# Seating the last two token tiles and placing gathered rows: a new order on TensorE between the dense and the expert products

## The chip, the cores and the metric

The kernel runs on one core of one Trainium2 chip. The metric is the device time of one execution in microseconds (us), as a median over several runs. The profile is of one execution of its own; its times are in us unless marked ns.

## What is computed

Three layers run one after the other over 1792 tokens of 768 features: attention with head mixing, a dense two-layer network, and a mixture of eight experts. The change stands where the second ends and the third begins:

```python
skip_score = x @ w_skip
do_compute = skip_score > 0
xc = x[do_compute]
logits = xc @ w_gate
e_idx = np.argmax(logits, axis=1)
gate_w = probs[np.arange(len(xc)), e_idx]        # softmax of the logits
for e in range(E):
    mask = e_idx == e
    h = np.maximum(xc[mask] @ w1[e], 0.0)
    y[mask] = gate_w[mask, None] * (h @ w2[e])
out[do_compute] = xc + y
```

Every token that computes goes to one expert, so each expert needs the list of its tokens before its products can start.

## The kernel before

**The dense products.** The 14 token tiles of 128 rows go through `w_out` tile by tile (L918). Tile 13 is LAST. Its 16 reduction steps are cut in two column halves near the end, so that the first 512 columns of its result are ready before the last 256. ScalarE copies each half out of PSUM into `x2` (L948).

**Scoring and routing.** Tiles 0 to 12 are scored on VectorE (`score`, L805). Tile 13 is turned by TensorE (`score_turned`, L903), copied by ScalarE (L904) and multiplied with the gate weights (`logits`, L894) into `lg`. `route` (L811 to L826) finds on VectorE the best expert (`oh`, one-hot, and `do`, whether the token computes) and the softmax weight; the exponential is ScalarE's (L824).

**Seating.** `seat` gives each token its place in its expert's list. TensorE multiplies `ones` with `seen`, the counts so far (L833), and `upper` with `oh` (L835), both into `pp`. VectorE adds `oh` to `seen` (L836), reads the place out of `pp` (`ps`, `sl`, L839), makes a slot number (`big`, `slot`, `si`), and GpSimd writes the token's number and weight into the table `slots` in DRAM (L853, an indirect DMA). OLD is 12: for tiles 12 and 13 `seat` also makes `hot` (L847), a 128 by 128 matrix that puts the tile's tokens straight into the first expert's input.

**Placing.** The input of expert 0 is gathered on TensorE in the PSUM tiles `pt`, in six column blocks k: rows of the tiles before OLD, which an indirect DMA has fetched into `xp` (L923), times `ident` (L889); rows of tile 12 times its `hot` (L890); rows of tile 13 times its `hot` (L963). `place_old` issues the first two for a block together. ScalarE and VectorE split `pt` into `xt0` (L965, L966), which the first expert product (L1113) reads.

**Experts.** `whi` and `wlo` are the high and low parts of the expert weights, made by ScalarE (L1084) and VectorE (L1086) from loads that SyncE issues (L1073). The products with `w1` are L1113, the turns of `h` L1101 to L1103, the products with `w2` L1126. GpSimd reads the lists back from `slots` into `ids` (L1237 to L1242) and gathers rows with them (L1091). `plan` counts the lists; `reorder` (L1050 to L1057) exchanges lists on VectorE after `ids` has landed.

**What sets the order.** In this part a scheduler orders each engine's queue at build time, by the order of the program, by what depends on what and by its own model of durations. `behind(op)` adds an edge that puts an instruction after `op` on the same engine's queue. At run time each engine works its queue off in that order.

Of the kernel before, what the change touches and what calls it, by code (L numbers as in the profile page):

```python
# [8 lines left out]
FP32 = mybir.dt.float32  # L9
# [4 lines left out]
ALU = mybir.AluOpType  # L14
# [6 lines left out]
NK = DM // 128  # L21
NF = DFF // 128
NTILE = NT // 128
# [464 lines left out]
def mixtures(tc, order, xT, w_in, w_out, w_skip, w_gate, w1, w2, ident, gT, wf, wg, x2d, slots, out):  # L488
# [5 lines left out]
    with ExitStack() as top:  # L494
# [266 lines left out]
        with ExitStack() as ctx:  # L761
# [47 lines left out]
            def route(i, lg):  # L809
# [14 lines left out]
                nc.scalar.activation(out=ex, in_=lg[:, :E], func=ACTF.Exp, bias=nmx, accum_out=sm)  # L824
                nc.vector.tensor_scalar(out=sm, in0=sm, scalar1=1e-9, scalar2=None, op0=ALU.add)
                nc.vector.reciprocal(out=pairs[:, i, 1:2].bitcast(FP32), in_=sm)  # L826
                return i, oh, do

            def seat(i, oh, do, after=None):

                pp = ps_r.tile([128, 512], FP32, tag="r", name="pp")
                with behind(after):
                    nc.tensor.matmul(out=pp[:, :E], lhsT=ones, rhs=seen, start=True, stop=False)  # L833
                with behind(after):
                    nc.tensor.matmul(out=pp[:, :E], lhsT=upper, rhs=oh, start=False, stop=True)  # L835
# [8 lines left out]
                place = None  # L844
                if i >= OLD:
                    place = wg_p.tile([128, 128], FP32, tag=f"hot{i}", name="hot")
                    nc.vector.tensor_scalar(out=place, in0=iota128, scalar1=sl, scalar2=do, op0=ALU.is_equal,  # L847
                                            op1=ALU.mult)
                slot = st_p.tile([128, 1], FP32, tag="slot", name="slot")
# [6 lines left out]
                return place  # L856

            gs = {0: load_g(0)}
            for f0 in range(EARLY, NF, 2):
# [23 lines left out]

            def place_old(ks):

                for k in ks:
                    col = slice(k * 128, (k + 1) * 128)
                    o = pt[k // 3][:, k % 3, :]
                    nc.tensor.matmul(out=o, lhsT=xp[:, col], rhs=ident, start=(k % 3 == 0), stop=False)  # L889
                    nc.tensor.matmul(out=o, lhsT=rows[LAST - 1][:, col], rhs=old_hot, start=False, stop=False)  # L890

            def logits(turned):
                for k, t in turned:
                    nc.tensor.matmul(out=lg[:, :E + 1], lhsT=t, rhs=wgt[:, k, :], start=(k == 0), stop=(k == NK - 1))  # L894

            def score_turned(x2, c):

                ks = range(0, CUT // 128) if c == 0 else range(CUT // 128, NK)
                p = ps_o.tile([128, 4, 128], FP32, tag=f"o{c}", name="tx")
                t = st_p.tile([128, 6, 128], FP32, tag="prod", name="tx", bufs=2)  # L900
                for j, k in enumerate(ks):
                    with behind(mm):
                        nc.tensor.transpose(p[:, j], x2[:, k * 128:(k + 1) * 128], ident)  # L903
                copied = nc.scalar.copy(out=t[:, :len(ks)], in_=p[:, :len(ks)])  # L904
                return [(k, t[:, j]) for j, k in enumerate(ks)], copied

            for i, n, fc, cs in work:
# [18 lines left out]
                if last and n == len(halves) - 5:  # L926
                    turned, _ = score_turned(x2, 0)
                if last and n == len(halves) - 3:
# [5 lines left out]
                if i and n == (AT_ROUTE if last else AT_OLD if i == OLD else AT_SEAT):  # L934
                    hot = old_hot = seat(*routing, None if last else mm)
                    if i == OLD:
# [482 lines left out]
```

## Time and profile before

| | |
|---|---|
| median of 3 runs | 993.32 us (992.25 to 994.23) |
| the profiled execution | 988.09 us |
| its span | 986.2 us |
| TensorE busy in the span | 963.5 us (98%) |
| VectorE busy | 722.0 us (73%) |
| ScalarE busy | 550.9 us (56%) |
| GpSimd busy | 233.5 us (24%) |

The span runs from the first to the last record of the profiled execution; 1.9 us of its time lie around it. Busy TensorE time includes matmuls that overlap, so it doesn't say how close the engine is to its peak.

### The profile page before, as it was taken

The numbers are of one execution on the slowest core, as the hardware profiler recorded it, in microseconds if no ns is written. First come the engines' busy times: TensorE is split into PE (matmuls) and PEld (weight loads), VectorE is DVE, ScalarE is ACT, GpSimd is POOL, SyncE is SP. The second block draws the span as 40 slices with busy tenths as digits, with TensorE's granted clock in tenths as the row PEclk, the third lists the DMA queues.
The fourth block names the chain that finished last, engine by engine and source line by source line (L and its number), as shares of the span: only waits on it lengthen the run. The fifth ranks groups of instructions, "written<-read, shape, count | busy, mean of one in ns | idle before, by whom it ended". The sixth has DMA issues, their size and how long they took to land. (4 is left out here: it accounts for less than half of the span.)

```text
span 986.2 us, 30114 instructions
## 1 busy us (share of the span) xinstructions
PE 963.5 (98%) x12286; PEld 838.7 (85%) x12286; DVE 722.0 (73%) x1458; ACT 550.9 (56%) x1113; POOL 233.5 (24%) x291
## 2 busy tenths in 40 slices
PE   9999999999998999999999999999999999999996
PEld 4677777777776789998999999999999998898985
DVE  6777777777776786666666478877686847999973
ACT  4887788788786754444554453222212106788861
POOL 2333234234222322223233100010100004252001
PEclk9999999999999999999999999999999999999999
DMA  6674674574557565445666389643333387999910
GB/s 202 219 237 145 216 234 156 198 240 153 195 190 234 175 207 184 157 161 169 219 225 211 137 292 290 175 126 97 118 97 100 104 294 264 394 394 397 391 71 34
DMA packets 129160, 199.86 MB, mean 203 GB/s; under 512 B 31924, under 2 KB 95863, under 8 KB 128764
## 3 DMA queue, kind: packets, MB, share of 16 engines
q1 hardware_dynamic: 126812, 191.60, 58.1%
q0 software_dynamic: 2160, 6.31, 1.7%
q8 instruction: 97, 1.59, 0.7%
q14 instruction: 43, 0.35, 0.1%
q10 hardware_dynamic: 48, 0.00, 0.0%
HBM read 122.66 MB, written 37.35 MB: 162 GB/s over the span
## 5 line engine op out<-in xcount | busy, mean ns | idle before, releaser
L918 PE MATMUL o<-w,gh 128*128 128x384 f32 (+2 forms) x1344 | 238.2, 336 | 0.0
L636 PE MATMUL h<-xh,w 128*128 128x448 f32 x1152 | 235.4, 366 | 1.6 <-DVE xh L572 1.3
L918 PEld LDWEIGHTS o<-w,gh 128*128 128x128 f32 x1344 | 232.0, 188 | 2.2
L636 PEld LDWEIGHTS h<-xh,w 128*128 128x128 f32 x1152 | 215.7, 188 | 20.2 <-DVE xh L572 1.9
L214 DVE TENSOR_REDUCE nmx<-c 128x1 f32<-128x448 f32 x184 | 102.3, 617 | 51.9 <-PE c L206 51.8
L266 PEld LDWEIGHTS f<-kr,e 64*64 64x64 f32 x5888 | 105.3, 135 | 36.6 <-issue 22.3
L227 ACT ACTIVATE e<-c,nmx 128x448 f32<-128x448 f32 x184 | 114.5, 633 | 25.5 <-DVE nmx L214 25.4
L805 DVE SCALAR_TENSOR_TENSOR junk<-x,wrow 128x768 f32<-128x768 f32 x117 | 111.8, 955 | 18.4 <-ACT x L948 12.8
L247 POOL TENSOR_SCALAR kr<-kpost,rs 128x60 f32<-128x60 f32 x184 | 79.4, 455 | 183.9 <-DVE rs L242 90.6
L1086 DVE TENSOR_TENSOR wlo<-w1t,whi 128x1536 fp32r<-128x1536 f32 x64 | 110.8, 1751 | 10.7 <-ACT whi L1084 8.9
L266 PE MATMUL f<-kr,e 64*64 64x60 f32 (+1 forms) x5888 | 108.3, 219 | 2.9 <-issue 1.8
L553 POOL TENSOR_TENSOR wf<-a,p 128x768 f32<-128x768 f32 x32 | 66.1, 2066 | 181.1 <-DVE p L551 139.4
L1084 ACT CAST whi<-w1t 128x1536 fp32r<-128x1536 f32 x64 | 93.8, 1483 | 21.5 <-PE y L1126 9.4
L790 ACT CAST gh<-gr 128x512 fp32r<-128x512 f32 x56 | 34.8, 624 | 97.1 <-PE o L918 35.5
L206 PE MATMUL c<-d,kpre_low 64*64 64x448 f32 x368 | 84.1, 547 | 0.3 <-DMA d<-s 0.2
L206 PE MATMUL c<-d,kpre_up 60*64 60x448 f32 x368 | 81.6, 548 | 0.0
L272 ACT COPY at<-f 128x420 f32<-128x420 f32 (+1 forms) x136 | 65.6, 518 | 28.0 <-PE f L266 27.2
L294 PE MATMUL xp<-at,v 128*64 128x120 f32 (+1 forms) x1152 | 67.1, 264 | 3.1 <-issue 3.0
L853 POOL DMA_INDIRECT slots<-pairs,si x14 | 18.9, 1348 | 204.6 <-DVE si L852 152.7
L166 PE MATMUL qk<-k,qq 64*120 64x448 f32 x504 | 65.3, 381 | 0.7 <-ACT e L227 0.2
L294 PEld LDWEIGHTS xp<-at,v 128*64 128x64 f32 x1152 | 56.1, 137 | 10.6 <-issue 9.3
L170 ACT ACTIVATE s<-qk 120x448 f32<-120x448 f32 x96 | 52.2, 548 | 23.1 <-PE qk L166 14.6
(204 smaller groups left out, 1278.7 us busy)
## 6 DMA issues: line engine op xcount, KB each, us to landing
w1t<-in_moe_w_dram SPq DMA_DIRECT2D x64, 768.0 KB
d<-s SPq DMA_DIRECT2D x176, 210.0 KB
gT<-g SPq DMA_DIRECT2D x64, 224.0 KB
f<-in_moe_w_in_dram SPq DMA_DIRECT2D x16, 768.0 KB
f<-in_moe_w_out_dram SPq DMA_DIRECT2D x16, 768.0 KB
gr<-gT SPq DMA_DIRECT2D x48, 256.0 KB
rq<-in_q_dram SPq DMA_DIRECT2D x15, 360.0 KB
rk<-in_k_dram SPq DMA_DIRECT2D x24, 224.0 KB
```

Source lines behind the costliest of these rows:

```text
L206: nc.tensor.matmul(out=ps[j * UP:(j + 1) * UP, :S], lhsT=kpre_up[UP:UP + HP, :] if z else kpre_low, rhs=d[z, j])
L214: nc.vector.tensor_reduce(out=t, in_=c, op=ALU.max, axis=AX.X, negate=True)
L227: nc.scalar.activation(out=e, in_=c, func=ACTF.Exp, bias=t, accum_out=sms[0][:, k + i:k + i + 1])
L247: nc.gpsimd.tensor_scalar(out=kr, in0=kposts[z], scalar1=rs[:, 2 * i + z:2 * i + z + 1], scalar2=None, op0=ALU.mult)
L266: nc.tensor.matmul(out=ps[to, heads, z, :], lhsT=e[rows, keys * JW:(keys + 1) * JW], rhs=kr[rows, first * HR:(first + n) * HR])
L294: nc.tensor.matmul(out=ps[i][z * 64:(z + 1) * 64, :n], lhsT=vt[b, p][:, jc * 2 + z, :], rhs=att[T][:, jc * H + ORDER.index(2 * p + z), :n] ...
L553: nc.gpsimd.tensor_tensor(out=w, in0=a, in1=p, op=ALU.add)
L636: nc.tensor.matmul(out=ps, lhsT=w[:, a, kk, :], rhs=xs[tb, kk][:, z, :], start=(kk == 0 and a + z == 0), stop=(kk == NK - 1 and a == 1))
L805: nc.vector.scalar_tensor_tensor(out=t[:, o:o + n], in0=x2, scalar=1.0, in1=w, op0=ALU.mult, op1=ALU.mult, accum_out=lg[:, e:e + 1])
L918: mm = nc.tensor.matmul(out=po[c][:, :cols[c].stop - cols[c].start], lhsT=gs[i][fc // GC][:, a, fc % GC, :], rhs=wo[fc][:, z, cols[c]], st ...
L1084: nc.scalar.copy(out=hi, in_=t)
L1086: nc.vector.tensor_tensor(out=lo, in0=t, in1=hi, op=ALU.subtract)
```

## The change

`place_old` is split: `place_pre` issues the products with `ident`, `place_old` those with the `hot` of tile 12. `seat` is split: `counted` issues the product of `ones` with `seen`, and for tile 12 the rest of `seat` is called later, between the turns and the logits of the last columns of tile 13. Edges fix one order on TensorE: `place_pre` of blocks 0 and 1, the turns, `upper` of tile 12, `place_pre` of blocks 2 and 3, the logits, `place_pre` of blocks 4 and 5, `place_old` of blocks 0 and 1, both products of tile 13's seat, `place_old` of blocks 2 to 5. On VectorE the two instructions of the softmax weight (`weigh`) stand behind `hot` for tiles 12 and 13, and the addition to `seen` stands after them in the program.

```diff
-                nc.vector.tensor_scalar(out=sm, in0=sm, scalar1=1e-9, scalar2=None, op0=ALU.add)
-                nc.vector.reciprocal(out=pairs[:, i, 1:2].bitcast(FP32), in_=sm)
-                return i, oh, do
+                def weigh(after=None):
+                    with behind(after):
+                        nc.vector.tensor_scalar(out=sm, in0=sm, scalar1=1e-9, scalar2=None, op0=ALU.add)
+                    nc.vector.reciprocal(out=pairs[:, i, 1:2].bitcast(FP32), in_=sm)
+                if i < OLD:
+                    weigh()
+                return i, oh, do, weigh
+            def counted(i, oh, do, weigh, after=None):
                 pp = ps_r.tile([128, 512], FP32, tag="r", name="pp")
                 with behind(after):
                     nc.tensor.matmul(out=pp[:, :E], lhsT=ones, rhs=seen, start=True, stop=False)
+                return i, oh, do, weigh, after, pp
...
-                nc.vector.tensor_tensor(out=seen, in0=seen, in1=oh, op=ALU.add)
                 nc.vector.scalar_tensor_tensor(out=ps, in0=pp[:, :E], scalar=1.0, in1=oh, op0=ALU.mult, op1=ALU.mult,
                                                accum_out=sl)
+                place = None
+                if i >= OLD:
+                    place = wg_p.tile([128, 128], FP32, tag=f"hot{i}", name="hot")
+                    made = nc.vector.tensor_scalar(out=place, in0=iota128, scalar1=sl, scalar2=do, op0=ALU.is_equal,
+                                                    op1=ALU.mult)
+                    weigh(made)
+                nc.vector.tensor_tensor(out=seen, in0=seen, in1=oh, op=ALU.add)
...
                         if last and c == 1:
-                            turned, freed = score_turned(x2, c)
-                            place_old(range(2))
-                            logits(turned)
-                            place_old(range(2, 4))
+                            placed = place_pre(range(2), mm)
+                            turned, freed, done = score_turned(x2, c, placed)
+                            with behind(done):
+                                done = seat_old()
+                            done = place_pre(range(2, 4), done)
+                            done = logits(turned, done)
+                            done = place_pre(range(4, NK), done)
+                            done = place_old(range(2), done)
...
-            hot = seat(*route(NTILE - 1, lg))
-            place_old(range(4, NK))
+            hot = seat(*route(NTILE - 1, lg), done)
+            place_old(range(2, NK), seated[LAST])
```

## Rows read from the trace of the kernel before

**Rows 1.** The page's head: span and number of instructions.

```profile
span 986.2 us, 30114 instructions
```

**Rows 2.** Busy time by stretch: PE, PEld, DVE, ACT, POOL, then clock, DMA share, GB/s.

```profile
836.00:977.00 141.00, 141.00 (x890) 126.52 (x889) 125.19 (x137) 101.91 (x102) 35.07 (x15) 1.00 0.78 297
815.70:822.75 7.05, 6.23 (x51) 5.54 (x49) 3.33 (x33) 3.23 (x8) 1.13 (x2) 1.00 0.64 245
```

**Rows 3.** Timeline of PE from the last dense product to the first expert product.

```profile
815.70 0.61 PE L889 MATMUL pt<-ident,xp 128*128 128x128 f32 x4
816.33 0.44 PE L903 MATMUL tx<-ident,x 128*128 128x128 f32 x2
817.23 0.61 PE L894 MATMUL lg<-wgt,tx 128*128 128x9 f32 x4 [0.46 <-ACT tx L904]
817.70 0.37 PE L835 MATMUL pp<-oh,upper 128*128 128x8 f32 x2
818.33 0.39 PE L833 MATMUL pp<-seen,ones 128*128 128x8 f32 x2 [0.27 <-DVE ps L839]
...
819.78 0.61 PE L890 MATMUL pt<-hot,x 128*128 128x128 f32 x4
820.23 0.29 PE L835 MATMUL pp<-oh,upper 128*128 128x8 f32 x2
...
821.35 1.50 PE L963 MATMUL pt<-hot,x 128*128 128x128 f32 x12
822.75 1.65 PE L1113 MATMUL ph<-whi,xt 128*128 128x512 f32 x6
```

**Rows 4.** Timeline of DVE: routing and seating of tiles 12 and 13.

```profile
815.39 0.17 DVE L811 MAX8 mx<-lg 128x8 f32<-128x8 f32 x1
...
816.06 0.28 DVE L819 TENSOR_SCALAR oh<-iota,ef,do 128x8 f32<-128x8 f32 x1
...
817.88 0.17 DVE L811 MAX8 mx<-lg 128x8 f32<-128x8 f32 x1 [1.53 <-PE lg L894]
...
818.41 0.33 DVE L847 TENSOR_SCALAR hot<-iota,sl,do 128x128 f32<-128x128 f32 x1
...
818.85 0.14 DVE L852 CAST si<-slot 128x1 int32<-128x1 f32 x1
...
818.97 0.29 DVE L819 TENSOR_SCALAR oh<-iota,ef,do 128x8 f32<-128x8 f32 x1
...
820.76 0.35 DVE L847 TENSOR_SCALAR hot<-iota,sl,do 128x128 f32<-128x128 f32 x1
```

**Rows 5.** Timeline of ACT in the same stretch.

```profile
816.80 0.37 ACT L904 COPY tx<-tx 128x256 f32<-128x256 f32 x1 [0.53 <-PE tx L903]
817.07 0.30 ACT L824 ACTIVATE ex<-lg,nmx 128x8 f32<-128x8 f32 x1
```

**Rows 6.** Timeline of POOL: writing the lists and reading them back.

```profile
819.27 1.02 POOL L853 DMA_INDIRECT slots<-pairs,si  x1 [3.47 <-DVE oh L819]
822.81 0.97 POOL L853 DMA_INDIRECT slots<-pairs,si  x1 [2.51 <-DMA slots<-pairs,si]
825.21 0.61 POOL L1237 DMA_DIRECT2D ids<-slots  x1 [1.43 <-DMA slots<-pairs,si]
...
826.91 0.90 POOL L1242 DMA_DIRECT2D ids<-slots  x1
```

**Rows 7.** Timeline of DVE and PE in the first expert's products.

```profile
829.40 1.74 DVE L1086 TENSOR_TENSOR wlo<-w1t,whi 128x1536 fp32r<-128x1536 f32 x1
...
832.45 0.17 DVE L1050 TENSOR_TENSOR swapped<-ids 128x8 int32<-128x8 int32 x1 [1.24 <-DMA ids<-slots]
832.53 1.75 DVE L1086 TENSOR_TENSOR wlo<-w1t,whi 128x1536 fp32r<-128x1536 f32 x1
...
834.27 0.68 DVE L1103 TENSOR_TENSOR ht<-pt,ht 128x512 fp32r<-128x512 f32 x1
...
835.00 1.66 PE L1126 MATMUL y<-whi,ht 128*128 128x384 f32 x8 [0.71 <-DVE ht L1103]
```

**Rows 8.** Timeline of SP: the first expert weight load after the seats.

```profile
825.69 0.38 SPq L1073 DMA_DIRECT2D w1t<-in_moe_w_dram  x1
```

More of the change, by code (lines that the diff above doesn't have):

```diff
@@ L824, in route @@
                 nc.scalar.activation(out=ex, in_=lg[:, :E], func=ACTF.Exp, bias=nmx, accum_out=sm)
-                nc.vector.tensor_scalar(out=sm, in0=sm, scalar1=1e-9, scalar2=None, op0=ALU.add)
-                nc.vector.reciprocal(out=pairs[:, i, 1:2].bitcast(FP32), in_=sm)
-                return i, oh, do
-            def seat(i, oh, do, after=None):
+                def weigh(after=None):
[6 more added lines that the diff above has]
+            def counted(i, oh, do, weigh, after=None):
                 pp = ps_r.tile([128, 512], FP32, tag="r", name="pp")
@@ L833, in seat @@
                     nc.tensor.matmul(out=pp[:, :E], lhsT=ones, rhs=seen, start=True, stop=False)
+                return i, oh, do, weigh, after, pp
+            def seat(i, oh, do, weigh, after=None, pp=None):
+                if pp is None:
+                    pp = counted(i, oh, do, weigh, after)[-1]
                 with behind(after):
-                    nc.tensor.matmul(out=pp[:, :E], lhsT=upper, rhs=oh, start=False, stop=True)
-                nc.vector.tensor_tensor(out=seen, in0=seen, in1=oh, op=ALU.add)
+                    seated[i] = nc.tensor.matmul(out=pp[:, :E], lhsT=upper, rhs=oh, start=False, stop=True)
                 ps = st_p.tile([128, E], FP32, tag="ps", name="ps")
@@ L843, in seat @@
                                         op1=ALU.add)
[L844 to L848, printed above, removed]
                 slot = st_p.tile([128, 1], FP32, tag="slot", name="slot")
@@ L856, in seat @@
                 return place
+            seated, started, hots = {}, [], []
             gs = {0: load_g(0)}
@@ L882, in mixtures, with place_pre, seat_old, place_old @@
             lg = ps_r.tile([128, 512], FP32, tag="r", name="lg")
-            def place_old(ks):
+            def place_pre(ks, after):
                 for k in ks:
[L887 to L892, printed above, removed]
-                for k, t in turned:
-                    nc.tensor.matmul(out=lg[:, :E + 1], lhsT=t, rhs=wgt[:, k, :], start=(k == 0), stop=(k == NK - 1))
-            def score_turned(x2, c):
+                    with behind(after):
+                        done = nc.tensor.matmul(out=pt[k // 3][:, k % 3, :], lhsT=xp[:, k * 128:(k + 1) * 128], rhs=ident,
+                                                start=(k % 3 == 0), stop=False)
+                return done
+            def seat_old():
+                hots.append(seat(*started[0]))
+                return seated[OLD]
+            def place_old(ks, after):
+                for k in ks:
+                    with behind(after):
+                        done = nc.tensor.matmul(out=pt[k // 3][:, k % 3, :],
+                                                lhsT=rows[LAST - 1][:, k * 128:(k + 1) * 128], rhs=hots[0],
+                                                start=False, stop=False)
+                return done
+            def logits(turned, after=None):
+                for k, t in turned:
+                    with behind(after):
+                        done = nc.tensor.matmul(out=lg[:, :E + 1], lhsT=t, rhs=wgt[:, k, :], start=(k == 0),
+                                                stop=(k == NK - 1))
+                return done
+            def score_turned(x2, c, mm):
                 ks = range(0, CUT // 128) if c == 0 else range(CUT // 128, NK)
@@ L902, in score_turned @@
                     with behind(mm):
-                        nc.tensor.transpose(p[:, j], x2[:, k * 128:(k + 1) * 128], ident)
+                        done = nc.tensor.transpose(p[:, j], x2[:, k * 128:(k + 1) * 128], ident)
                 copied = nc.scalar.copy(out=t[:, :len(ks)], in_=p[:, :len(ks)])
-                return [(k, t[:, j]) for j, k in enumerate(ks)], copied
+                return [(k, t[:, j]) for j, k in enumerate(ks)], copied, done
             for i, n, fc, cs in work:
@@ L926, in mixtures @@
                 if last and n == len(halves) - 5:
-                    turned, _ = score_turned(x2, 0)
+                    turned, _, _ = score_turned(x2, 0, mm)
                 if last and n == len(halves) - 3:
@@ L934, in mixtures @@
                 if i and n == (AT_ROUTE if last else AT_OLD if i == OLD else AT_SEAT):
-                    hot = old_hot = seat(*routing, None if last else mm)
+                    if last:
+                        started.append(counted(*routing, mm))
+                    else:
+                        seat(*routing, mm)
                     if i == OLD:
```

## The prediction

> **What bounds the kernel now.** I read the page first for the span, 986.2 us [rows 1]; with the 1.9 us around it that execution took 988.09 us, and all sums below are against it. The runs' median is 993.32 us, 5.23 us more; I carry a difference over to it unchanged.
>
> Next I read busy time by stretch. From 836 to 977 us TensorE is busy in 141.00 of 141.00 us, at the full granted clock [rows 2]; among the waits of that stretch none is TensorE's. The expert products thus run back to back, and whatever moves their start moves the end by as much, as long as VectorE (125.19 us busy) keeps ahead. The changed stretch, 815.70 to 822.75 us, lasts 7.05 us with TensorE busy in 6.23 [rows 2]. This is a small target: even with no pause at all in it, less than 2 us could be won there.
>
> Then I followed the stretch in the timelines, engine by engine. The reader is to see three holes in TensorE's queue: it waits for the copied turns until 817.23, it waits for `ps` of tile 12 until 818.33, and `upper` of tile 13 starts only at 820.23 [rows 3] though its `oh` was there at 819.26 [rows 4]. That last one is not a wait; `upper` stands in the queue behind the placing products. The last view is the stretch behind: there GpSimd's list traffic [rows 6] reaches VectorE's queue, and at 835.00 TensorE waits 0.71 us for it [rows 7].
>
> **The work itself.** Nothing is removed or added on TensorE: 12 passes with `ident`, 12 with the first `hot`, 12 with the second, and the seats' eight stay. Passes start 0.11 us apart: four from 819.78 to 820.23 [rows 3]. VectorE has the same instructions too, and so has GpSimd. Only order changes.
>
> **TensorE's order, step by step.** `place_pre` of blocks 0 and 1 stays where it is (815.70), and so do the turns (816.33), which wait for ScalarE's copy. They end their issue 2 x 0.11 later, at 816.55. Then come `upper` of tile 12 (its `oh` is there at 816.34 [rows 4]), 0.22, and `place_pre` of blocks 2 and 3, four passes, 0.44: until 817.21. The copy that the logits need ends at 817.17 [rows 5], so these six passes fit into the hole, and the logits start at 817.23 as before. They cost nothing while that copy covers them; if it came 0.4 us earlier, they would cost up to 0.4.
>
> Logits end as before, and VectorE starts `MAX8` of tile 13 at 817.88. From `MAX8` to the end of `oh` it takes 0.95 us for tile 12, where little stands between (815.39 to 816.34), and 1.38 for tile 13 (817.88 to 819.26), where seat 12's instructions are mixed in [rows 4]. In the new order `hot` of tile 12 is made in the idle 1.53 us ahead of `MAX8`, but the weight's two instructions and the slot's stay near it. So `oh` of tile 13 is ready between 818.83 and 819.26. TensorE meanwhile has: logits from 817.23, four passes, 817.70; `place_pre` of 4 and 5 to 818.14; `place_old` of 0 and 1 to 818.58; `ones` to 818.80. It is ready for `upper` of tile 13 just before, so `upper` starts at 818.88 to 819.31, against 820.23. Behind it, by the new edge, stand eight passes of `place_old`: 0.22 + 0.88 = 1.10, and L963 starts at 819.98 to 820.41. The second `hot` is no bar: it ended 0.88 us after `upper` started (820.23 to 821.11 [rows 3, 4]), so it is there at 819.76 to 820.19.
>
> L963 started at 821.35: **0.94 to 1.37 us earlier**, I take 1.2, nearer to the short chain since `hot` 12 has left it. From L963 to the first expert product is 1.40 us (821.35 to 822.75 [rows 3]), set by the split of `pt`, unchanged.
>
> **The lists, which move less.** The gain has to pass 835. There VectorE's queue holds `reorder`'s first instruction, L1050, which stood 1.24 us waiting for `ids` until 832.45; behind it stand `wlo` (1.75) and the low part of `ht` (L1103), and for that TensorE waits 0.71 at 835.00 [rows 7]. What releases L1050 is not TensorE but the chain on GpSimd: write of list 12 at 819.27, write of list 13 at 822.81 after the first has landed, reading back from 825.21, the last read at 826.91 [rows 6], landed at 832.45.
>
> When can that chain start? `si` of tile 12 ended at 818.99 and GpSimd started 0.28 later [rows 4, 6]. In the new order `ps` 12 follows `upper` 12 (816.55) by about 0.32, `hot` ends near 817.4; the weight needs ScalarE's exponential, started at 817.07 [rows 5] and read by about 817.5; then six short instructions of 0.07 to 0.19 us each with `MAX8` among them: `si` 12 ends at 818.2 to 818.6. The write starts at 818.5 to 818.9, **0.4 to 0.8 us earlier**, I take 0.7. List 13 is not the bar: it waited 2.51 us for the landing of list 12 [rows 6], and its own `si` moves forward with `upper`.
>
> The rows show the price of a landing: 2.51 us after the end of the first write's record, 1.43 after the second's [rows 6]. The Trainium skill, page "DMA: Bandwidth & Descriptors", section "Anatomy of one DMA — SWDGE (gpsimd) path", says that such a DMA costs a fixed 2.0 us or so whatever its size, most of it the receipt from the memory written; the trace agrees in kind, at 1.43 to 2.51 us. By that rule, too, nothing in this chain gets shorter, only its start moves.
>
> So the products arrive at 835 with 1.2 us in hand, VectorE's wait at L1050 grows from 1.24 to about 1.7, and of the 1.2 us only what the lists gained goes on: **0.7 us**. TensorE's stop grows from 0.71 to about 1.2. Behind it nothing waits until 977, so the end moves by 0.7: 988.09 - 0.7 = 987.4 for the profiled kind of run, 993.32 - 0.7 = 992.6 for the median.
>
> The weight's move behind `hot` costs nothing for tile 13 (its list waits for list 12 anyway); for tile 12 it is in the sum. `seen` of tile 12 must be added before `ones` at 818.58; it follows `hot` 12 by three short instructions, about 818.0.
>
> **Rivals.**
>
> *The whole advance arrives.* The scheduler orders VectorE's queue anew, and if L1050 stands behind the next `wlo`, or the lists start as early as the products, the stop at 835 no longer eats anything. Then 1.2 us arrive, or with the 0.71 of the stop also gone about 1.9: 992.1 to 991.4. For it: the order there is the scheduler's, not the program's. Against: L1050's wait is already there before, so its model puts the landing earlier than it is. The Trainium skill, page "Perfetto Trace Analysis", section "Identifying Performance Opportunities", counsels to work on the gaps of the most contended engine; by that, TensorE's own 1.2 us would be the gain. The row of the wait at L1050 speaks for less.
>
> *Nothing arrives.* Weight loads start when VectorE has freed a buffer; the first was at 825.69 [rows 8]. It moves forward by 1.2, the lists' reads by 0.7, so more of the loads' traffic is under way when the last read is issued. If that read lands 0.7 later for it, the lists have won nothing: 993.3. The same holds if `si` 12 is not earlier, because VectorE's order puts it behind `MAX8` and its followers.
>
> *L1050 moves ahead of a `wlo`: slower.* Since list 12 is seated earlier in the program, the scheduler may place L1050 before the `wlo` of 829.40 [rows 7]. Then that 1.74 us piece waits for the landing too: it would start at 831.8 instead of 828.2 (829.40 - 1.2), and TensorE, which used it 1.2 us after its start, would stop for about 3.6 us, less the 1.2 in hand and the stop at 835 that it replaces (0.71): 1.7 us slower, and 2 to 3 with the piece behind it late: 995.0 to 996.3. It decides as soon as L1050 stands before that `wlo` and the lists land after 829.5. Against it: VectorE's order there is otherwise given by the same readiness as before.
>
> *The change does not do what it says*: if `oh` 12 or the fetched rows came late, the new edges would hold the logits. `oh` 12 is there 0.2 us ahead [rows 4]; I give it little.
>
> **Chances.** Forecast (0.4 to 1.0 us faster) 0.5; the whole advance 0.25; nothing 0.13; slower by L1050 or a similar order 0.1; edges that hold the logits 0.02. Of the whole advance a little less than half may exceed the 0.2% (1.99 us) that a measurement of this kernel can tell, when both the stop and the three holes go: 0.1. Of the slower cases 0.07 exceed it. So faster 0.1, same 0.83, slower 0.07. The range runs from the whole advance with the stop gone (991.4, less 0.5 for the runs' own spread) to a small loss of 0.7 with the same kind of spread: 990.9 to 994.3; the likeliest case alone is 992.0 to 993.2.
>
> **What would show it.** Right: `upper` 12 between the turns and the logits near 816.6; the logits still at 817.2; `upper` 13 near 819.0; L1113 near 821.6; the first list write near 818.6; L1050 still waiting, longer than before, until about 831.8; TensorE's stop before the `w2` products about 1.2 us. Wrong: logits later than 817.3, a list write after 819.0, L1050 at another place in VectorE's queue, or any wait of TensorE between 836 and 977.

## The result, and the profile after

The changed kernel takes 997.75 us (988.25 to 1003.09, 20 executions) against 991.15 us of the kernel before beside it (986.54 to 1003.07, 20 executions): ratio 1.006, from 1.0037 to 1.0083. It is slower, by 6.6 us in the medians; 992.6 was forecast, and 994.3 was the range's upper end.

First the page's head, and busy time by stretch (PE, PEld, DVE, ACT, POOL, clock, DMA share, GB/s): the changed stretch, and the products behind the stop.

```profile
span 991.5 us, 30115 instructions
```

```profile
821.39:827.21 5.82, 5.80 (x51) 5.49 (x49) 3.56 (x33) 3.13 (x8) 1.12 (x2) 1.00 0.83 315
841.90:982.00 140.10, 140.10 (x883) 125.88 (x885) 124.47 (x137) 100.67 (x101) 35.05 (x15) 1.00 0.78 296
```

The timeline of PE in the changed stretch and at the first stop behind it:

```profile
821.39 0.61 PE L901 MATMUL pt<-ident,xp 128*128 128x128 f32 x4
822.01 0.44 PE L933 MATMUL tx<-ident,x 128*128 128x128 f32 x2
822.29 0.29 PE L846 MATMUL pp<-oh,upper 128*128 128x8 f32 x2
822.43 0.69 PE L901 MATMUL pt<-ident,xp 128*128 128x128 f32 x4
822.96 0.57 PE L922 MATMUL lg<-wgt,tx 128*128 128x9 f32 x4
...
824.59 0.39 PE L846 MATMUL pp<-oh,upper 128*128 128x8 f32 x2
...
825.80 1.50 PE L1000 MATMUL pt<-hot,x 128*128 128x128 f32 x12
827.21 1.64 PE L1150 MATMUL ph<-whi,xt 128*128 128x512 f32 x6
...
840.25 1.68 PE L1163 MATMUL y<-whi,ht 128*128 128x384 f32 x8 [1.52 <-DVE ht L1140]
```

The timeline of POOL, DVE and SP from the list writes to that stop (L865 is L853 of before, L1123 is L1086, L1087 is L1050, L1110 is L1073):

```profile
824.13 1.02 POOL L865 DMA_INDIRECT slots<-pairs,si  x1 [2.65 <-DVE nmx L821]
...
828.33 3.48 DVE L1123 TENSOR_TENSOR wlo<-w1t,whi 128x1536 fp32r<-128x1536 f32 x2
828.35 0.98 POOL L865 DMA_INDIRECT slots<-pairs,si  x1 [3.19 <-DVE xt L1003]
...
830.20 0.38 SPq L1110 DMA_DIRECT2D w1t<-in_moe_w_dram  x1
...
830.76 0.61 POOL L1274 DMA_DIRECT2D ids<-slots  x1 [1.43 <-DMA slots<-pairs,si]
...
837.69 0.17 DVE L1087 TENSOR_TENSOR swapped<-ids 128x8 int32<-128x8 int32 x1 [2.05 <-DMA ids<-slots]
...
839.51 0.68 DVE L1140 TENSOR_TENSOR ht<-pt,ht 128x512 fp32r<-128x512 f32 x1
```

From here all places are counted from the first placing product (L889 before, L901 after) and written t+; the time "to the end" is the span less that product's start. The changed stretch did what was forecast: first expert product at t+5.82 (827.21 - 821.39) against t+7.05 [rows 2, 3], 1.23 us earlier, with `upper` of tile 12 between the turns and the logits and TensorE busy in 5.80 of 5.82 us.

Behind it the picture differs from the forecast in three rows. The first list write moved forward by 0.83 us (t+2.74 against t+3.57 [rows 6]), but the second only by 0.15 (t+6.96 against t+7.11): it waits for the first to land, and that now takes 3.19 us instead of 2.51. (The row names VectorE's `xt`, but the write reads `si` and `pairs`, both done by 825.90, and in before and e4 the same wait is put down to the landing.) The first `wlo` starts at t+6.94, next to that second write; it stood at t+8.17 before, 1.06 us behind it. And the first later load, t+8.81, now goes ahead of the first list read, t+9.37; before, the read was ahead, 825.21 against 825.69 [rows 6, 8]. TensorE's stop grew from 0.71 [rows 7] to 1.52.

None of this gives 6.6 us: this execution takes 170.11 us from the first placing product to the end, against 170.50 (986.2 - 815.70) before. The same kernel has a second course of events, and this execution did not take it. A later profiled execution of it (e17) took 1003.14 us, 178.83 of them to the end. Its timeline of DVE, POOL, SP and PE:

```profile
829.51 3.42 DVE L1123 TENSOR_TENSOR wlo<-w1t,whi 128x1536 fp32r<-128x1536 f32 x2
829.60 2.52 POOL L865 DMA_INDIRECT slots<-pairs,si  x1 [3.26 <-DVE xt L1003]
...
831.32 0.38 SPq L1110 DMA_DIRECT2D w1t<-in_moe_w_dram  x1
...
836.13 0.61 POOL L1274 DMA_DIRECT2D ids<-slots  x1 [4.01 <-DMA slots<-pairs,si]
...
845.43 0.17 DVE L1087 TENSOR_TENSOR swapped<-ids 128x8 int32<-128x8 int32 x1 [8.55 <-DMA ids<-slots]
...
847.98 2.29 PE L1163 MATMUL y<-whi,ht 128*128 128x384 f32 x6 [8.03 <-DVE ht L1140]
```

And its busy time by stretch (columns as above), during the stop and behind it:

```profile
842.57:847.57 5.00, 0.00 (x0) 0.00 (x0) 2.14 (x4) 0.27 (x1) 2.82 (x3) 0.51 1.05 377
847.57:852.57 5.00, 4.59 (x14) 4.59 (x15) 5.00 (x18) 0.34 (x1) 1.69 (x2) 0.50 0.58 204
```

The reader is to see a chain. The second list write starts 0.09 us behind the start of `wlo` instead of 0.02, and takes 2.52 us instead of 0.98. It is done at 832.12, behind the load of 831.32, and lands 4.01 us after its end instead of 1.43. The first list read is issued at t+13.56 instead of t+9.37, `swapped` waits 8.55 us with `wlo` and `ht` queued behind it, TensorE stops 8.03 us, and the granted clock is at 0.50 to 0.51, the lower of its two levels (1.2 GHz), in the two stretches shown, 10 us together.

### The profile page after: what moved, and what is told of

Read it like the earlier page. It is cut to its first block, busy times and chain, and to the rows that moved or that the text cites. A ratio compares the mean times of both kernels' runs of the same rounds, so it can differ in the third digit from the quotient of the medians.

```text
span 991.5 us, 30115 instructions
## 1 busy us (share of the span) xinstructions
PE 966.4 (97%) x12286; PEld 842.1 (85%) x12286; DVE 721.8 (73%) x1458; ACT 550.4 (56%) x1113; POOL 232.1 (23%) x291
## 5 line engine op out<-in xcount | busy, mean ns | idle before, releaser
L1123 DVE TENSOR_TENSOR wlo<-w1t,whi 128x1536 fp32r<-128x1536 f32 x64 | 110.9, 1752 | 10.4 <-ACT whi L1121 8.3
L865 POOL DMA_INDIRECT slots<-pairs,si x14 | 18.9, 1348 | 204.3 <-DVE si L864 154.1
```

The lines of the kernel that those rows point to most:

```text
L1123: nc.vector.tensor_tensor(out=lo, in0=t, in1=hi, op=ALU.subtract)
```

## The experiments

What each profiled execution shows, in us (write: the second list write's start and duration; clock: the lowest mean granted in the slices t+10 to 15, t+15 to 20 and so on to t+45; a short fall that lies across two slices shows as two smaller ones, as in e2):

| | write at, takes | first read | first later load | `swapped` | stop ahead of `w2` | clock | to the end |
|---|---|---|---|---|---|---|---|
| before | 7.11, 0.97 | 9.51 | 9.99 | 16.75 | 0.71 | 1.00 | 170.50 |
| e1, before again | 7.10, 0.98 | 9.52 | 11.61 | 17.07 | none | 1.00, but 0.84 in t+0 to 5, 0.82 in t+5 to 10 | 171.18 |
| e6, before, gather late | 6.61, 0.98 | 9.02 | 9.98 | 16.30 | 0.24 | 1.00 | 170.08 |
| e7, before, reads on SyncE | 7.37, 0.97 | 9.54 | 11.48 | 16.94 | none | 1.00, but 0.78 in t+0 to 5, 0.88 in t+5 to 10 | 170.96 |
| after | 6.96, 0.98 | 9.37 | 8.81 | 16.30 | 1.52 | 1.00 | 170.11 |
| e2, after again | 6.85, 0.98 | 9.27 | 8.76 | 16.56 | 1.77 | 0.73 | 171.96 |
| e8, after again | 7.10, 2.43 | 13.55 | 8.75 | 22.28 | 7.48 | 0.60 | 177.36 |
| e16, after again | 6.68, 0.97 | 9.08 | 8.76 | 16.51 | 1.73 | 1.00 | 170.34 |
| e17, after again | 7.03, 2.52 | 13.56 | 8.75 | 22.86 | 8.03 | 0.50 | 178.83 |
| e18, after again | 6.96, 0.98 | 9.37 | 8.81 | 16.50 | 1.70 | 1.00 | 170.50 |
| e9, before, write late | 8.60, 2.23 | 15.26 | 10.05 | 23.62 | 7.57 | 0.57 | 178.77 |
| e14, e9 and load held | 8.59, 2.23 | 12.26 | 12.38 | 20.12 | 4.09 | 0.66 | 176.25 |
| e10, after, `wlo` later | 6.37, 0.97 | 8.78 | 9.11 | 16.09 | 1.27 | 1.00 | 169.97 |
| e13, after, `wlo` gated | 6.91, 0.98 | 9.32 | 9.92 | 17.36 | 1.88 | 0.66 | 172.67 |
| e11, after, load held | 6.82, 0.97 | 9.23 | 9.35 | 16.78 | 1.96 | 0.66 | 172.00 |
| e3, after, `swapped` later | 6.65, 0.98 | 9.07 | 8.76 | 17.54 | 1.48, on ScalarE | 1.00 | 170.46 |
| e4, after, store later | 5.77, 0.98 | 8.19 | 8.75 | 16.36 | 11.64, on ScalarE | 0.50 | 181.23 |
| e5, after, reads on SyncE | 7.10, 2.44 | 10.73 | 12.60 | 14.25 | none | 1.00 | 168.76 |
| e12, the same | 7.74, 1.78 | 10.72 | 12.59 | 14.24 | none | 1.00 | 168.38 |
| e15, the same | 6.48, 0.97 | 8.64 | 10.51 | 14.21 | none | 1.00 | 168.30 |

### Is it chance, or a loss ahead of the change? e1 and e2

The kernel before and the changed kernel, both unaltered, on one chip. The first theories were drawn from the profiled executions alone: a loss in front of the changed stretch (the first placing product stood at 821.39 us instead of 815.70), or the larger stop.

> The kernel before, unchanged, timed against itself. Theory A (chance): the attention stretch, ahead of 340 us, takes a different time in every execution, by several us, whatever stands behind 815 us; then the ratio is 1.000 with an interval about as wide as that of the change (+-0.2 to 0.4%), single times scatter over 10 us or more, and the profile's times ahead of 340 us differ from the first profile's by 1 to 6 us. Theory B (the changed program itself slows the stretches ahead): the same spread here is small, within 2 us, and the ratio is 1.000 +-0.1%. From the last dense product to the end both expect 170.5 us, as in the first profile, +-0.2.

> The changed kernel, unchanged. Theory A: the ratio is 0.997 to 1.003, as the local effect is -0.4 us and the rest was chance. Theory B: the ratio is 1.004 to 1.008 again, and the profile loses 4 to 6 us ahead of 340 us against the null run. From the last dense product to the end both expect 170.1 us +-0.2.

e1: 993.7 us, ratio 0.9989 (0.9958 to 1.0021). e2: 995.57 us, ratio 1.0026 (0.9993 to 1.0058). A loss in front is not seen as a cause: over the six profiled executions with the old order the first placing product stands between 815.70 and 824.82 us, 821.4 in the mean; over the fourteen executions with the new order between 817.74 and 828.23, 821.5 in the mean. That time varies from execution to execution by more than the change is worth. A difference of 1 or 2 us in front would not show in so few profiles; e5, e12 and e15 below, which keep the new order and are faster than the kernel before, speak against it.

e1 shows one thing more. The granted clock fell in the changed stretch itself, to 0.50 from 824.72 to 827.22 us, and the first `w2` products came at t+18.57 instead of t+16.93 in the kernel before, so `swapped` at t+17.07 no longer kept TensorE waiting: no stop. e7 shows the same fall (0.50 from 826.94 to 829.44). So the old order loses by the clock in two of its six profiled executions, and the new one in none of its fourteen: both slices from t+0 to t+10 are at 1.00 in all of them.

### The wait at `swapped`, and the stores: e3 and e4

e3 puts `swapped` behind the first low part of `ht` (`lows` holds these parts in order), and the seventh `wlo` with it; e4 puts the store of tile 13's rows behind five of the later loads:

```diff
+                with behind(lows[0]):
+                    nc.vector.tensor_tensor(out=d[:, :n - 1], in0=idt[:, PAIR:E - 1],
+                                            in1=idt[:, E - 1:E].to_broadcast([128, n - 1, 2]), op=ALU.bitwise_xor)
...
-                with behind(routed if early else None):
+                with behind(routed if early else lows[0] if n_parts[0] == 7 else None):
```

> The changed kernel with the first instruction of reorder behind the low part of ht on VectorE, and the seventh wlo behind it too. Theory of the gate (the 1.2 us won on TensorE stop at VectorE's wait for the lists): the 1.5 us stop ahead of the w2 products goes, and from the last dense product to the end it takes 168.6 to 169.3 us instead of 170.1. Rival (TensorE is held there by ScalarE's and VectorE's casts anyway): the stop stays over 1 us, with wlo or h in place of ids as the releaser, and the stretch stays at 170.0 +-0.3. For the total: theory A gives 0.996 to 1.002, theory B 1.003 to 1.008.

```diff
-            nc.sync.dma_start(out=out[LAST * 128:, :], in_=x2)
...
+            with behind(loads[W_EARLY]):
+                nc.sync.dma_start(out=out[LAST * 128:, :], in_=x2)
```

> The changed kernel with the store of tile 13's rows to the output (384 KB) moved from ahead of the lists to behind five of the later weight loads. Theory of the traffic (list 12 cannot land before the transfers issued ahead of it have drained): the landing of list 12 comes 0.7 to 1.0 us earlier against the last dense product, the wait of reorder and the stop of TensorE shrink by as much, to 0.5 to 0.9 us, and the stretch to the end takes 169.2 to 169.6 us. Rival (the landing is a fixed latency): list 12 lands 3.2 us after its issue's end as before, nothing moves, 170.1.

e3: 997.94 us, ratio 1.0045 (1.0008 to 1.0082); to the end 170.46. The scheduler moved the second turn of `h` too, and TensorE stopped 1.48 us at `w2` for ScalarE and 0.93 us at the turn of the gathered rows. The wait at `swapped` was gone and nothing was won.

e4: 1001.43 us, ratio 1.0088 (1.0054 to 1.0122); a stop of 11.64 us for ScalarE's copy into `ht`, which itself stood idle 8.98 us; probably `ht` takes the buffer of tile 13's rows and now waits for the moved store, but the trace names no releaser. As a version it is spoilt, but it points to what holds the landing of the first list: it landed 2.00 us after its record instead of 3.19, and the second write started at t+5.77 instead of t+6.96. In no other profile with the new order did that landing take less than 2.60.

### The gather, or the list reads? e5 to e8

In the profiled execution of the changed kernel the first gather of rows is issued at t+14.80 instead of t+12.41. e5 (from the changed kernel) and e7 (from the kernel before) move all four list reads to SyncE, ahead of the later loads; e6 gives the kernel before a late first gather, by five fills behind the four list reads; e8 is the changed kernel again. For e5 and e7, one of the reads and the loads:

```diff
-            nc.gpsimd.dma_start(out=idt[:, 1:2], in_=by_expert[:, 1:2])
+            nc.sync.dma_start(out=idt[:, 1:2], in_=by_expert[:, 1:2])
...
+            lists = nc.sync.dma_start(out=idt[:, 3:E], in_=by_expert[:, 3:])
...
-                    with behind(wrow_in if len(raws) < R0 else None):
+                    with behind(wrow_in if len(raws) < R0 else lists if len(raws) > R0 + RA + RB + RC else None):
```

For e6:

```diff
-            xg[1] = gather(ids[1])
...
-                xg[e] = gather(ids[e])
...
+            read = nc.gpsimd.dma_start(out=idt[:, 3:E], in_=by_expert[:, 3:])
...
+            with behind(read):
+                for _ in range(5):
+                    idled = nc.gpsimd.memset(idle, 0.0)
+            with behind(idled):
+                for e in (1, 0, 2):
+                    xg[e] = gather(ids[e])
```

> The changed kernel with the four list reads issued on SyncE's queue, ahead of the weight loads that wait for freed buffers, instead of on GpSimd behind them. Gather theory (the slowdown comes from the list reads falling behind the first later weight load, so that the first gather of rows is issued 2.4 us later while TensorE asks for it 0.4 us earlier): the first gather is issued 12.5 us or less after the first placing product instead of 14.8, the ratio to the kernel before falls to 0.997 to 1.000. Front theory (the loss lies ahead of the changed stretch and has nothing to do with the lists): 1.004 to 1.006 as before. Clock theory (TensorE's stop ahead of the w2 products and the lower clock behind it): back to 1.000 only if that stop shrinks to 0.8 us or less; with the stop at 1.5 or more, 1.003 to 1.006.

> The kernel before, with five fills of a scratch tile (128x512 each, about 0.5 us) on GpSimd between the list reads and the first gather, so that the first gather is issued at about 14.8 us after the first placing product instead of 12.4. Nothing else moves. Gather theory: slower by 2.5 to 5 us, ratio 1.003 to 1.006, with a stop of TensorE at the turn of the gathered rows in some executions. Clock and front theories: 0.998 to 1.002.

> The kernel before, with its list reads on SyncE's queue as in the first run of this batch. Gather theory: the lists were not late in it, so at most the stop of 0.71 us ahead of the w2 products goes: 0.998 to 1.000. Clock theory: 0.997 to 1.000. Front theory: 1.000.

> The changed kernel once more, unaltered, beside the others on the same chip. All theories: 1.003 to 1.006 to the kernel before. Its trace is one more draw: the gather theory expects, in a slow execution, a stop of TensorE at the turn of the gathered rows; the front theory expects the loss ahead of the first placing product; the clock theory a granted clock below 0.7 right behind the stop at the w2 products.

e6: 990.96 us, ratio 0.9987 (0.9954 to 1.002), with its gather at t+14.89. The gather theory falls: no cost of that lateness is seen. e5: 990.29 us, 0.9978 (0.9947 to 1.0008), while e8 took 997.98 us, 1.0025 (0.9986 to 1.0063). e7: 992.29 us, 0.9998 (0.9975 to 1.0022). So the loss goes when the list reads leave GpSimd's queue and the loads wait for them (e5 does both at once), and it isn't the gather behind them. e8's profiled execution shows where it was: the long second write and the stop of 7.48 us. From it comes the port theory: a list write that starts while VectorE works on a `wlo` takes 2.4 us, and its transfer then falls behind a weight load.

### The long write made on purpose: e9 and e14

e9 is the kernel before with one VectorE instruction moved: the conversion `si` of tile 13 behind the second split of `pt`. Up to TensorE's stop the instructions of all queues otherwise stand in the same order in the two profiles. e14 is e9 with a read of one list row on SyncE ahead of the later loads, so that these wait for the write's landing.

For e9, with `write` called at once for the other tiles, and for tile 13 after the loop over `xt0`:

```diff
+                def write(after=None):
+                    with behind(after):
+                        nc.vector.tensor_copy(out=si, in_=slot)
+                    nc.gpsimd.indirect_dma_start(out=slots, out_offset=bass.IndirectOffsetOnAxis(ap=si[:, 0:1], axis=0),
...
+            writes[0](routed)
```

For e14 besides:

```diff
+            landed = nc.sync.dma_start(out=tiny, in_=slots[0:1, :])
...
-                    with behind(wrow_in if len(raws) < R0 else None):
+                    with behind(wrow_in if len(raws) < R0 else landed if len(raws) > R0 + RA + RB + RC else None):
```

> The kernel before, with one instruction moved: the conversion of tile 13's list positions (si) stands behind the second split of pt instead of ahead of the first, so that the second list write is issued about 0.3 us behind the start of the first long low part (wlo) instead of 1.1 us ahead of it; it starts about 1.5 us later. Port theory (a list write that starts within a wlo takes 2.4 us instead of 1.0, its transfer then falls behind the first later weight load and lands 4 us behind its record instead of 1.4): the write takes 2.3 to 2.5 us, the first list read is issued at about 15 us after the first placing product instead of 9.5, TensorE stops 6 to 9 us ahead of the w2 products, in nearly every execution; ratio 1.005 to 1.010. Delay theory (lists that come 1.5 us later cost 1.5 us): ratio 1.000 to 1.002, stop 2.2 us.

> The kernel of e9 (the kernel before with its second list write started within a wlo) with the later weight loads held on SyncE until that write has landed. If the load ahead of the write is what turns 1.3 us into 4: the write takes 2.2 us and lands 1.4 to 2 us behind its record, the reads are issued at about 12.3 us, TensorE stops 2 to 4 us ahead of the w2 products; ratio 1.002 to 1.005 instead of 1.0128. If the long write alone costs the time: 1.010 or more.

e9: 1003.44 us (998.5 to 1011.02), ratio 1.0128 (1.0075 to 1.0181), more than expected. The timeline of DVE and POOL, and the row of TensorE's waits (line and releaser, us in total, times, longest):

```profile
829.87 3.42 DVE L1095 TENSOR_TENSOR wlo<-w1t,whi 128x1536 fp32r<-128x1536 f32 x2
830.23 2.23 POOL L856 DMA_INDIRECT slots<-pairs,si  x1 [4.00 <-DVE si L855]
...
836.89 0.61 POOL L1246 DMA_DIRECT2D ids<-slots  x1 [4.43 <-DMA slots<-pairs,si]
```

```profile
PE y L1135 <- DVE ht L1112: 7.6, 1, 7.6
```

e14: 997.78 us, ratio 1.0061 (1.0036 to 1.0085), with the same long write. The timeline of POOL and SP, and the row of the waits:

```profile
829.94 2.23 POOL L856 DMA_INDIRECT slots<-pairs,si  x1 [4.00 <-DVE si L855]
...
833.37 0.25 SPq L1246 DMA_DIRECT2D tiny<-slots  x1
...
833.61 0.61 POOL L1248 DMA_DIRECT2D ids<-slots  x1 [1.43 <-DMA slots<-pairs,si]
...
833.73 0.38 SPq L1082 DMA_DIRECT2D w1t<-in_moe_w_dram  x1
```

```profile
PE y L1135 <- DVE ht L1112: 4.1, 1, 4.1
```

This separates the halves. With no load ahead of it the write lands 1.43 us after its end, with one ahead of it 4.43; that is 3.00 us, and 2.52 of them (178.77 - 176.25) reach the end. The rest, 5.75 us against before (176.25 - 170.50), belongs to the write itself, which starts 1.48 us later and takes 1.26 longer, and to the clock: the stop of 4.09 is followed by 0.66. The delay theory, 1.5 us in all with a stop of 2.2, falls; what the later start alone would cost, with no `wlo` in the way, no run shows.

### Keeping the write clear in the changed kernel: e10, e11, e13

e10 fills 128x384 on VectorE ahead of the first `wlo` (first diff); e13 holds this `wlo` until GpSimd has done the write (second diff); e11 holds the later loads as e14 does, and leaves `wlo`.

```diff
+            with behind(routed):
+                routed = nc.vector.memset(xp[:, :384], 0.0)
```

```diff
+            with behind(wrote[LAST]):
+                nc.gpsimd.memset(gate, 0.0)
+            with behind(routed):
+                routed = nc.vector.tensor_copy(out=xp[:, :1], in_=gate)
```

> The changed kernel with a fill of 128x384 (about 0.4 us) on VectorE between the second split of pt and the first wlo, so that this wlo starts at about 7.3 us after the first placing product instead of 6.94, behind the second list write (6.85 to 7.10) in all executions. It adds work and removes none. Port theory: the write takes 1.0 us in all executions, the executions of 997 us and more go; ratio 0.997 to 1.001. Any theory by which the changed order is slower of itself, or the lists only shift with their start: 1.003 to 1.006 or a little more.

> The changed kernel, with a read of one list row on SyncE ahead of the later weight loads: the loads wait until the second list write has landed. The list reads stay on GpSimd and the first wlo stays where it is, so the write may still take 2.4 us. Port theory with the load as its second half: the write's landing takes 1.4 us again even where the write took 2.4, the reads are issued at 9.4 or 11, the executions of 997 us and more go; ratio 0.997 to 1.001. If the long write alone does the harm: 1.002 to 1.005.

> The changed kernel with the first wlo on VectorE held until GpSimd has written the descriptors of the second list write (a fill of one column on GpSimd behind that write, and a copy of it on VectorE ahead of the first wlo). Port theory: the write takes 1.0 us in every execution, no execution at 998 us or more, ratio 0.997 to 1.001. If the long write is not the cause of the slow executions in the changed kernel: 1.003 to 1.006, with some 4 in 10 executions at 998 us or more as in e10.

e10: 994.68 us, ratio 1.004 (1.0007 to 1.0074), against 0.997 to 1.001 expected: a miss. The expectation took the write's start for 6.85 to 7.10; e12 shows one at t+7.74, behind this kernel's `wlo` at t+7.35 too. That e10's slower executions had such a write isn't shown, since its profiled one did not. e13: 993.16 us, 1.0026 (0.9995 to 1.0056), between what the two theories expected; four of its twelve executions took 998 us or more, and none was expected. Its profiled execution, 1002.7 us, has the write short, the read ahead of the load, and still a stop of 1.88 us with the clock at 0.66 behind it (172.67 to the end); the other part of its length lies in front, with the first placing product at 828.23. The hold is not free: the first `wlo` starts at t+8.11 instead of t+6.94, and TensorE stops 0.41 us for it. e11: 994.8 us, 1.0031 (1.0001 to 1.0062), with a stop of 1.96 and the clock at 0.66.

So the long write is not all of the loss. In e2, e13 and e11 the stops of 1.77, 1.88 and 1.96 us are followed by a stretch at a lower granted clock, and e2 shows its price: 1.85 us more to the end than after, for a stop 0.25 longer, so 1.6 us beyond the stop. What is left of the stop in e11 and e13, with the write short, the next section takes up.

### The changed kernel with its lists read first: e12 and e15

> The kernel of e5 once more (list reads on SyncE ahead of the later weight loads), to tell whether it beats the kernel before: e5 had 0.9978, from 0.9947 to 1.0008. Port theory: no execution at 997 us or more, 0.996 to 0.999. If e5 was a lucky draw: 1.000 to 1.004.

> The kernel of e5 and e12 a third time: 0.996 to 0.999 again if the change is worth its 1.2 us and the stop of 0.71 once the lists are read ahead of the later loads; 1.000 or more if the first two were draws.

e12: 989.18 us, ratio 0.9976 (0.9943 to 1.0009). e15: 989.28 us, 0.9969 (0.9942 to 0.9996). e12's timeline of DVE, POOL and SP, and all that its view of TensorE's waits lists behind 815 us:

```profile
824.96 3.42 DVE L1123 TENSOR_TENSOR wlo<-w1t,whi 128x1536 fp32r<-128x1536 f32 x2
...
825.76 1.78 POOL L865 DMA_INDIRECT slots<-pairs,si  x1 [3.98 <-DVE xt L1003]
...
828.74 0.33 SPq L1274 DMA_DIRECT2D ids<-slots  x1
...
830.51 1.74 DVE L1123 TENSOR_TENSOR wlo<-w1t,whi 128x1536 fp32r<-128x1536 f32 x1
830.61 0.46 SPq L1110 DMA_DIRECT2D w1t<-in_moe_w_dram  x1
...
831.36 1.75 POOL L1128 DMA_INDIRECT xg<-x2d,ids  x1 [3.81 <-DMA ids<-slots]
...
832.26 0.17 DVE L1087 TENSOR_TENSOR swapped<-ids 128x8 int32<-128x8 int32 x1
```

```profile
PE pt L1138 <- ACT h L1156: 0.3, 1, 0.3
```

`swapped` doesn't wait, the stop at `w2` is gone, and that although the write started late and within a `wlo`. What differs is the landing of the reads. In e11 the last one ends its record on GpSimd at t+11.82 with two loads issued ahead of it, and `swapped` starts at t+16.78, 4.96 us later; before it is 4.64, after 4.34. In e5 and e12 all four reads go ahead of the later loads, the last ends at t+12.49 and t+12.48, and `swapped` finds them landed 1.76 us later. So, as far as these runs show, the stop comes of the loads that are under way when the lists are read, and the long write puts one more link of the chain behind them. Over e5, e12 and e15 the 36 executions take 989.93 us in the mean and none reaches 997. Of 128 executions of the kernel before, timed beside the experiments, 14 do (992.36 in the mean), of 44 of the changed kernel 23 (996.39). This version is the fastest of the three, by 2.4 and 6.5 us in the mean. The lists on SyncE alone (e7, 0.9998) do not show that gain, though e7's own interval is 0.2% wide on either side; the order on TensorE brings the rest once they are out of the way.

### How often: e16, e17, e18

> The changed kernel unaltered, one profiled execution. Port theory: the second list write starts between 6.4 and 7.8 us after the first placing product; where it starts after 6.95 it takes 1.8 us or more, the first list read is issued at 12 us or later, and the rest to the end takes 175 us or more; where it starts before, it takes 1.0, the read is issued at 9 to 9.5 and the rest takes 170 to 172.5.

> A second look at the changed kernel unaltered, with the same two cases: a write of 1.0 us and 170 to 172.5 us to the end, or a write of 1.8 us or more and 175 us or more.

> A third look at the changed kernel unaltered, with the same two cases: a write of 1.0 us and 170 to 172.5 us to the end, or a write of 1.8 us or more and 175 us or more.

992.09, 1003.14 and 994.65 us, each as one of the two cases. Of six profiled executions of the changed kernel two had the long write (177.36 and 178.83 us to the end), four the short one (170.11 to 171.96). Their mean, 173.18, lies 2.3 us above that of the two of the kernel before (170.84); the executions' means differ by 4.0. Six are too few to settle the share of long writes.

The mean granted clock of every execution is a rough sign of it: it was 0.990 and 0.989 in the two with the long write, 0.994 to 0.997 in the other four. At 0.992 or below were 20 of the 44 executions of the changed kernel, 11 of the 128 of the kernel before, all 6 of e9, 6 of 12 of e10, 4 of 12 of e14, 1 of 12 of e13 and 1 of the 36 of e5, e12 and e15. So the long write is probably nearer to one execution in two than to one in three; e10 seems not to have kept it away, e13 to have done so, and three of e13's four executions over 998 us, at 0.993 to 0.995, were then long for another reason. A sign is not a trace (e13's one execution below 0.992 is its profiled one, with a short write), so the size of the loss is explained in kind, not to the microsecond.

## Why the prediction was wrong

**TensorE's order: right.** 0.94 to 1.37 us were forecast for the stretch, 1.2 taken, 1.23 measured; every place in it came within 0.2 us of the working.

**The list chain's start: right at its first link, wrong at the second.** The first write was to move by 0.4 to 0.8, and moved by 0.83. The prediction then moved the whole chain by that. But the second write waits for the landing of the first, and this didn't keep its 2.51 us: it took 3.19 and left 0.15. e4 points to the store of tile 13's rows as the bar (2.00 with it out of the way). The sentence that "list 13 is not the bar" was true, and the landing of list 12 was taken for a constant.

**The failed step: "The lists, which move less".** It took the landings over from the kernel before as fixed prices, 2.51 and 1.43 us for the writes and the time to 832.45 for the reads, while two other things moved past the chain by 1.2 us: the first `wlo` on VectorE and the first later load on SyncE. Before, the second write stood 1.06 us ahead of the first and its read 0.48 ahead of the second. After, it meets the one within 0.1 us and its read comes behind the other. The step asked when the chain starts, and not what starts beside it. In e17 the landing that was taken at 1.43 took 4.01, behind a write of 2.52 instead of 0.97, and TensorE's stop was 8.03 us where 1.2 were forecast. In e9 the write within a `wlo` is made in the kernel before: 8.3 us more to the end (178.77 - 170.50), with a start 1.5 us later in it.

**The rival "Nothing arrives" named the place and mis-sized the price.** It saw the loads move by 1.2 and the reads by less, priced the collision at 0.7 us, to end at no gain, and gave it 0.13. What collides is the write, a link earlier, and the price is 3.00 us (e9 against e14), with the write's own 1.5 and the clock on top. No rival had the write and `wlo` together.

**"L1050 moves ahead of a `wlo`" did not happen**; the order on VectorE stayed. The harm it described, a `wlo` held up by the landing, came all the same, by a later landing instead of an earlier place.

**"Behind it nothing waits until 977" was right for waits** (140.10 of 140.10 us busy) and left out the clock: the stop was forecast at about 1.2, where no fall is seen (e10, 1.27), but it was 1.52 to 1.77 with the short write, 7.48 and 8.03 with the long one, and behind the longer ones the clock fell.

**"The whole advance arrives"** was worth 1.9 us with the stop gone. It is what e5, e12 and e15 do: 170.50 to 168.48 in the mean to the end, 2.0 us.

**The range.** Its upper end, 994.3, is 0.2 below its own terms (993.32 + 0.7 + 0.5 = 994.5); the measured 997.75 lies above both. The carry from one profiled execution to the median was also a gap: the profile of before shows one of two courses (e1 shows the other), and so does the profile after.

**A rule that was there to be read.** GpSimd's indirect transfers are held up by a running `wlo`, and the trace of the kernel before shows it already, in the timelines of DVE and POOL:

```profile
827.59 1.75 DVE L1086 TENSOR_TENSOR wlo<-w1t,whi 128x1536 fp32r<-128x1536 f32 x1
828.11 2.11 POOL L1091 DMA_INDIRECT xg<-x2d,ids  x1 [0.30 <-issue]
```

This gather starts within the `wlo` and ends at 830.22, 0.88 us after the end of it (829.34). The other rows agree: e17's write ends at 832.12, the first of its two `wlo` at about 831.26 (829.51 + 1.75), 0.86 us before; e12's gather starts 0.85 us into a `wlo` that ends at 832.25, and ends at 833.11, again 0.86 later. Those list writes and gathers that meet none take 0.94 to 1.03. The Trainium skill, page "SBUF — State Buffer", section "SBUF: two separate sides", says that VectorE and GpSimd share a pair of ports under an exclusive lock, and that an operation of VectorE with two inputs in SBUF holds it against an operation of GpSimd that reads SBUF. That a transfer issued from GpSimd is stalled by this lock it says of VectorE's two-port modes, and advises to issue it from another queue. The trace agrees that `wlo`, with both inputs in SBUF, holds up the indirect writes and gathers (e17's write took 2.52 us); the plain list reads on GpSimd took their 0.61 us within a `wlo` too (at 825.21 [rows 6]). That the lock is what holds them, no run here shows. By these rows a moved `wlo` is a term of the sum, and the prediction had none for it.

## What to carry to other kernels

When a change moves one engine's work forward, list all that this work releases on other engines (here a `wlo` and, through the buffer that it frees, a weight load), and look for what these now pass: an order that held by a margin of 0.5 to 1 us before is a term of the sum, even if no wait shows it. A landing is not a constant; ask what else is in the queues when it starts. And where one execution of the profile shows no loss but the median does, look at more executions before looking at more engines: the loss here lay in a second course of events that one profile in three shows.

## What was not expected of the hardware

A list write that starts 0.02 us behind the start of a `wlo` took 0.98 us, one that starts 0.09 us behind it 2.52. A gather can be held by more than one: in e12 the one at 849.12, 0.35 us ahead of a row of six `wlo`, took 11.83 us and ended 0.84 us after the last of them; in e1 one that started 0.39 us ahead of a `wlo` took 0.97. The same small write landed 1.43 us after its end with no weight load ahead of it, and 4.01 to 4.43 us with one. TensorE's granted clock stayed at full speed behind the stops of 1.27 to 1.73 us ahead of `w2`; it went to its lower level behind those of 1.77, 1.88 and 1.96 (0.50 from 841.64 to 844.14 in e2) and behind or within those of 4.09 to 11.64. The length of a stop alone does not decide it: behind two holes of 0.46 and 0.26 us in the old order it fell in e1 and e7 and stayed at full speed in before, e6, e9 and e14, where the holes were the same within 0.01.
